# Windowed attention and two MLPs: in the last Winograd sweep ScalarE copies both accumulator banks, an adding DMA joins them in DRAM, and the plan gets new lengths and a new order

## The chip, the cores and the metric

The kernel runs on one core of a Trainium2 chip. The metric is the device time of one execution in microseconds. Before the change it was 630.57 us (median of three runs, 630.27 to 630.82).

## What is computed

Three stages follow each other over 2304 tokens (4 sequences of 576) of 512 features, in float32:

```python
scores = scale * q @ k.T                       # 4 x 8 heads, 576 x 576, 64 per head
attn   = softmax(where(0 <= i - j < 64, scores, -1e9)) @ v
x      = attn as (2304, 512)
h      = maximum(x @ w_in, 0);  x = (h * h) @ w_out          # FFN1, 512 -> 2048 -> 512
h      = x @ w2_in                                           # FFN2, 512 -> 1024
solu   = h * softmax(h)
ln     = (solu - mean) / sqrt(var + 1e-6) * g_ln
out    = ln @ w2_out                                         # 1024 -> 512
```

## The kernel before

Every float32 product is made as three products of a high and a low part, so one block product is some multiple of three matmuls. FFN1 runs in passes over the tokens. The first pass multiplies plainly. The second and the last use Strassen-Winograd: seven half-size products in place of eight, with sums and differences of the operands made by VectorE (DVE).

**The last pass.** For each j of eight, the products of the first layer are followed by the parts of the second layer whose operands are at hand: P1, P2 and P4. The operands of the other four products are stored in DRAM. When the first layer is done, `swept()` runs the sweep: P5 (8 steps), P6 (8), P3 (8) and P7 (8). A step is six matmuls of 128x512. Its operand is read back from DRAM (line 1199 is the load), copied by ScalarE (ACT) as the high part (line 1091), subtracted by DVE for the low part (line 1094) and multiplied at line 1070. P1, P6 and P7 accumulate in one pair of PSUM banks ("b"), P5 and P3 in another ("a"), P4 in a third ("t"), P2 in a fourth.

**What leaves the sweep.** The four quarters of the result are sums of banks: c11 is P1 + P2, c12 is the P5/P3 bank plus a saved copy U2 of the P1/P6 bank, c21 is the P1/P6/P7 bank plus P4, and c22 is that bank plus a saved copy of P5. `out()` does it: ACT copies one bank to SBUF (line 1152, or `copied` at line 1174 for the saved ones), DVE adds the other bank to that copy (line 1157, eight adds in all), and SyncE (SP) stores the sum (line 1160). P6 continues in the banks of P1, so its first matmul waits until c11 has been added. The t banks of P4 are given back when c21 has been added, which is after P7.

**FFN2.** `pair2(n)` does nine pairs of token tiles, again by Winograd: seven products of six matmuls (line 1546), whose banks ACT copies (u2 at 1556, u4 at 1560, u5 at 1564; `xx` at 1521 are high parts of the operands), then softmax, LayerNorm and transposes through DRAM (`lnT`, lines 1696 and 1700), then 48 matmuls at line 1707. Pair 0 takes the a banks, pair 1 the t banks, pair 2 the b banks. The variance's root is taken by GpSimd (POOL, lines 1652 and 1653).

**What sets the order.** Nothing is left to a scheduler of the compiler. Each task is put into a `Plan` with an engine, a planned length, a rank, the buffers that it takes and gives, and a lateness (`late`: the time from the end of a DMA's issue to its planned landing). The plan lists the tasks by earliest start, then by rank; `SHIFT` corrects ranks by task number, and each engine gets its instructions in the order so found. 51 dummy matmuls ("warm", line 1782) of rank 900 fill what the plan sees as gaps of TensorE (PE).

Of the kernel before, what the change touches and what calls it, by code (L numbers as in the profile page):

```python
# [26 lines left out]
class Plan:  # L27
# [10 lines left out]
    SHIFT = {0: 13.59, 3: 4.48, 4: -11.32, 22: -7.17, 37: 14.79, 71: -15.08, 162: -5.57, 188: 6.06, 192: -3.28, 195: 10.82, 198: 10.82, 202: -1.28,  # L38
# [69 lines left out]
def kernel(  # L108
# [96 lines left out]
    with ExitStack() as c1:  # L205
# [20 lines left out]
        tops, turns = [], [0]  # L226

        def assembled(kind, i, rank, after=()):
# [22 lines left out]
            def top():  # L251
                if ringed:
# [593 lines left out]
        def w_operands(t, j, rank, after):  # L846
# [59 lines left out]
            kept_wo[j] = [add("SP", 1.6, rank + WOS, lambda o=o, k=k: kept(o, k), [x], late=2.5) for k, (o, x) in enumerate(((V_, v), (Y, y)))]  # L906
# [929 lines left out]
```

## Time and profile before

| | |
|---|---|
| median of three runs | 630.57 us |
| the profiled execution | 631.49 us |
| its span | 629.7 us |
| PE busy | 621.6 us |
| DVE busy | 484.6 us |
| ACT busy | 434.8 us |
| POOL busy | 45.3 us |

The profiled execution is 0.92 us above the median; its span leaves 1.8 us outside. In the rows further down, times are microseconds from the start of the span. A row of a timeline begins with the start and the duration of a run of like instructions, then engine, line, operation, tiles and count; a bracket at the end is the idle time ahead of it and what ended that. Consecutive matmuls overlap, so the pace of PE is read from start to start. L1070 is line 1070 of the code above.

### The profile page before, as it was taken

To read this page: it belongs to the slowest core of one execution; us is meant where nothing else is said; L and a number is where in the kernel's file an instruction comes from. 1 tells how busy PE (TensorE), PEld (TensorE's weight loads), DVE (VectorE), ACT (ScalarE), POOL (GpSimd) and SP (SyncE) were. 2 spreads that over 40 slices of the span, in tenths; PEclk is the share of its full clock that TensorE was granted. 3 is DMA by queue.
4 is the path that set the end of the run, shared out by engine and by line. 5 is a ranking of instruction groups with operands and counts; after the bars stand their busy time and mean duration, and the time that the engine had idled before them with its cause. 6 is when DMAs were issued, how large, how long until landed. Compare 5 with 4: busy or idle time off the path is not lost.

```text
span 629.7 us, 11572 instructions
## 1 busy us (share of the span) xinstructions
PE 621.6 (99%) x4009; PEld 523.7 (83%) x4009; DVE 484.6 (77%) x1129; ACT 434.8 (69%) x985; POOL 45.3 (7%) x80
## 2 busy tenths in 40 slices
PE   8999999999999999999999999999999999999998
PEld 4798878889999999998888887778778788888886
DVE  5999897497967652587899998998688976686440
ACT  5879785677877674638677767774688875776451
POOL 1000000001221110000000000000001010110010
DMA  8888979447899998946767557964166565532351
GB/s 274 287 305 278 310 252 326 128 173 264 247 351 312 336 304 271 337 155 230 236 251 263 203 195 235 328 208 138 68 184 206 181 199 167 197 137 86 116 184 50
DMA packets 85451, 141.27 MB, mean 224 GB/s; under 512 B 7824, under 2 KB 49552, under 8 KB 85392
## 3 DMA queue, kind: packets, MB, share of 16 engines
q1 hardware_dynamic: 84704, 140.14, 66.3%
q8 instruction: 31, 0.51, 0.3%
q10 hardware_dynamic: 688, 0.39, 0.2%
q14 instruction: 28, 0.23, 0.1%
HBM read 90.69 MB, written 49.81 MB: 223 GB/s over the span
## 4 chain that ended last, share of the span: by engine, by line
PE 86%; DVE 5%; DMA 4%; ACT 3%; issue 1%; SPq 1%; POOL 0%; ACTq 0%; DVEq 0%; POOLq 0%
PE ps_h L936 22%; PE ps_o L1707 14%; PE ps_y L1070 10%; PE ps_h L1546 10%; PE ps_y L1256 10%; PE ps_y L707 7%; PE ps_h L691 6%; PE ps_s L436 3%; PE ps_v L519 2%; PE ps_warm L1782 1%; DMA l<-t_dram 1%; DMA kt<-in_k 1%; DMA r_dram<-u 1%; DMA t_dram<-h 1%; PE ps_v L522 1%
## 5 line engine op out<-in xcount | busy, mean ns | idle before, releaser
L1707 PE MATMUL ps_o<-w2o,lnT 128*128 128x512 f32 x432 | 99.1, 389 | 0.0
L1707 PEld LDWEIGHTS ps_o<-w2o,lnT 128*128 128x128 f32 x432 | 81.1, 188 | 16.9
L1256 PE MATMUL ps_y<-g,wb 128*128 128x384 f32 x384 | 71.3, 336 | 0.4 <-ACT y L655 0.4
L1256 PEld LDWEIGHTS ps_y<-g,wb 128*128 128x128 f32 x384 | 66.6, 188 | 1.4 <-ACT y L655 0.7
L1546 PE MATMUL ps_h<-w2i,xx 128*128 128x512 f32 x243 | 62.8, 391 | 0.0
L1070 PE MATMUL ps_y<-g,wb 128*128 128x512 f32 x234 | 58.3, 391 | 1.1 <-DVE y L1157 1.0
L1546 PEld LDWEIGHTS ps_h<-w2i,xx 128*128 128x128 f32 x243 | 45.6, 188 | 9.6
L1070 PEld LDWEIGHTS ps_y<-g,wb 128*128 128x128 f32 x234 | 43.7, 188 | 11.4 <-DVE y L1157 1.4
L936 PE MATMUL ps_h<-xa,wo 128*128 128x512 f32 (+1 forms) x192 | 52.7, 369 | 0.0
L936 PE MATMUL ps_h<-xb,wo 128*128 128x384 f32 (+1 forms) x192 | 51.3, 358 | 0.0
L707 PE MATMUL ps_y<-g,wb 128*128 128x512 f32 (+1 forms) x240 | 48.2, 352 | 0.1
L691 PE MATMUL ps_h<-x,wa 128*128 128x512 f32 (+1 forms) x240 | 47.3, 351 | 0.0
L936 PE MATMUL ps_h<-xo,wo 128*128 128x512 f32 (+1 forms) x128 | 47.3, 369 | 0.0
L451 ACT ACTIVATE e<-e,nmax 128x128 f32<-128x128 f32 x112 | 43.3, 390 | 2.2 <-DVE nmax L440 2.2
L707 PEld LDWEIGHTS ps_y<-g,wb 128*128 128x128 f32 x240 | 38.5, 189 | 6.6 <-issue 0.7
L691 PEld LDWEIGHTS ps_h<-x,wa 128*128 128x128 f32 x240 | 38.5, 189 | 6.0 <-ACT g L637 0.2
L936 PEld LDWEIGHTS ps_h<-xa,wo 128*128 128x128 f32 x192 | 35.3, 188 | 5.2 <-DVE u L622 0.4
L1696 ACT ACTIVATE lnT<-l 128x512 fp32r<-128x512 f32 x36 | 22.2, 627 | 23.0 <-PE ps_o L1707 23.0
L1546 PE MATMUL ps_h<-w2x,xx 128*128 128x512 f32 x135 | 37.0, 393 | 0.9 <-ACT u L1560 0.7
L936 PEld LDWEIGHTS ps_h<-xb,wo 128*128 128x128 f32 x192 | 34.5, 188 | 3.9 <-issue 0.7
L640 DVE TENSOR_TENSOR g<-r,g 128x384 fp32r<-128x384 f32 (+2 forms) x36 | 20.4, 570 | 21.7 <-ACT g L637 21.7
L461 POOL TENSOR_TENSOR e<-e,sums 128x512 f32<-128x512 f32 x16 | 18.5, 1179 | 205.0 <-PE ps_h L936 141.9
(182 smaller groups left out, 1267.7 us busy)
## 6 DMA issues: line engine op xcount, KB each, us to landing
wraw<-in_w_in SPq DMA_DIRECT2D x24, 511.8 KB, 5.3
wraw<-in_w_out SPq DMA_DIRECT2D x24, 511.8 KB, 4.8
vt<-in_v SPq DMA_DIRECT2D x32, 256.0 KB, 4.3
wo_dram<-wo SPq DMA_DIRECT2D x16, 512.0 KB, 5.4
wo<-wo_dram SPq DMA_DIRECT2D x16, 512.0 KB, 4.9
t_dram<-h SPq DMA_DIRECT2D x16, 512.0 KB, 2.9
l<-t_dram SPq DMA_DIRECT2D x64, 128.0 KB, 2.9
kt<-in_k SPq DMA_DIRECT2D x16, 384.0 KB, 5.2
```

Source lines behind the costliest of these rows:

```text
L436: T.matmul(to, qt[rows, i, hp, :], kt[rows, keys, hp, :], start=not begins, stop=not begins or hp == hps[-1])
L451: S.activation(out=o["er"][:, a, w], in_=s, func=AF.Exp, scale=SCALE if begins else -1.0, bias=o["nmax"][:, a, w : w + 1], accum_out=o["su ...
L461: eng.tensor_tensor(out=o["er"][:, a], in0=o["er"][:, a], in1=o["sums"][:, a].unsqueeze(2).to_broadcast([P, HP, W]), op=ALU.mult)
L640: V.tensor_tensor(out=o["g"][:, 1, :N], in0=o["r"], in1=o["g"][:, 0, :N].bitcast(F32), op=ALU.subtract)
L691: T.matmul(ps[:, :N], wa[kk][:, wi, c * P : c * P + P], xs[t][:, xi, c, n0:n1], start=n == 0, stop=n == 3 * DC - 1)
L707: T.matmul(acc[t, 0][d][:, n0:n1], wb[kk][:, wi, d * P : d * P + P], o["g"][:, xi, :N], start=kk == 0 and n == 0 and n0 == 0, stop=last an ...
L936: T.matmul(to[:, :N], w["t"][:, wi, off + c * P : off + c * P + P], (lo if xi else hi)()[:, c], start=begins and m == 0, stop=m == 5, skip ...
L1070: T.matmul(acc[name][d][:, :N], wb[kk][:, wi, col + d * P : col + d * P + P], q["g"][:, xi, :N], start=j == 0 and n == 0 and name not in ( ...
L1256: T.matmul(acc[t, half][d][:, :N], wb[kk][:, wi, d * P : d * P + P], q["g"][:, xi, :N], start=pos == 0 and n == 0, stop=pos == KF - 1 and ...
L1546: T.matmul(o[bank], o["xx", k][:, xi, at : at + P], w2i[w, r][wi][0](), start=begins and m == 0, stop=m == 5, skip_group_check=True)
L1696: S.activation(out=parts2(o["l", hf][:, 0]), in_=turned2(hf), func=AF.Copy)
L1707: T.matmul(o["o"], o["l", hf][:, xi, kk % 4, :], w2o[kk][:, wi, :], start=kk == 0 and n == 0, stop=kk == KF2 - 1 and n == 2)
```

## The change

`out()` is replaced by three helpers. `taken()` lets ACT copy a bank to SBUF. `stored_as()` lets SP store such a copy plainly to its place in DRAM. `added_to()` lets POOL issue a DMA with `accum_op=ALU.add`, which adds the other copy to what lies there; it comes after the plain store has landed. All eight DVE adds vanish, ACT copies 14 banks where it copied 8, SP still issues eight stores, and POOL issues eight adding transfers of 128x512. The banks of P4 are given back as soon as ACT has copied them. Five planned latenesses grow, the two halves of a zeroed buffer (`top`) are handed out in the order in which they come free, and `SHIFT` is a new table, so that the plan comes out in another order nearly everywhere.

```diff
-    SHIFT = {0: 13.59, 3: 4.48, 4: -11.32, 22: -7.17, 37: 14.79, 71: -15.08, ...
+    SHIFT = {0: 13.59, 10: -12.41, 22: -7.17, 27: -14.74, 28: -9.14, ...
...
-        tops, turns = [], [0]
+        tops, turns = [], [0, 1]
...
-            kept_wo[j] = [add("SP", 1.6, rank + WOS, lambda o=o, k=k: kept(o, k), [x], late=2.5) ...
+            kept_wo[j] = [add("SP", 1.6, rank + WOS, lambda o=o, k=k: kept(o, k), [x], late=3.0) ...
...
-                r_ready[t, kk] = add("SP", 0.8, ..., late=LATE_R if t == 2 else 2.2, give=["wm"])
+                r_ready[t, kk] = add("SP", 0.8, ..., late=LATE_R + 0.45 if t == 2 else 2.2, give=["wm"])
...
-            kept_t[j, "T1"] = ... late=2.2 ...; kept_t[j, "B22"] = ... late=2.2 ...; kept_t[j, "T"] = ... late=2.5 ...
+            kept_t[j, "T1"] = ... late=2.65 ...; kept_t[j, "B22"] = ... late=2.65 ...; kept_t[j, "T"] = ... late=3.4 ...
...
-            def out(d, half, a, b, after, early=None, **kw):
+            def taken(bank, after, rank, **kw):
                 o = {}
                 def copy():
                     o["y"] = raw_p.tile([P, 512], F32, tag="wm", name="y", bufs=WMB)[:, :N]
-                    S.activation(out=o["y"], in_=b(), func=AF.Copy)
-                def evict():
...
-                    V.tensor_tensor(out=o["y"], in0=a(), in1=b() if early is None else o["y"], op=ALU.add)
-                def store():
-                    nc.sync.dma_start(out=x2_dram[t][:, d, half * N : half * N + N], in_=o["y"])
...
-                y = add("DVE", 0.68, r, evict, after, take=["wm"] * (early is None), **kw)
+                    S.activation(out=o["y"], in_=bank(), func=AF.Copy)
+                return o, add("ACT", 0.58, rank, copy, after, take=["wm"], **kw)
+            def stored_as(d, half, y, after, slot=("wm",)):
+                def store():
+                    nc.sync.dma_start(out=column(d, half), in_=y())
+                return add("SP", 0.8, begin + 50, store, after, late=2.2, give=list(slot))
+            def added_to(d, half, o, after, slot=("wm",)):
+                def grow():
+                    G.dma_start(out=column(d, half), in_=o["y"], accum_op=ALU.add)
+                stored.setdefault((t, half), []).append(add("POOL", 1.1, begin, grow, after, late=5.5, give=list(slot)))
...
-            c11 = [out(d, 0, bank_of("P1", d), bank_of("P2", d), done, done[1:], rank=begin - 20, give=["b"] * d) for d in range(2)]
+            for d in range(2):
+                o, e = taken(bank_of("P2", d), done[1:], begin - 20)
+                first.append(stored_as(d, 0, lambda o=o: o["y"], [e]))
+            for d in range(2):
+                o, e = taken(bank_of("P1", d), [*done, e], begin - 20, give=["b"] * d)
+                c11.append(e)
+                added_to(d, 0, o, [e, first[d]])
...
-            ys = [out(2 + d, 0, bank_of("P1", d), bank_of("P4", d), [p7], [p7, into["P4", last]], rank=begin, give=["t"]) for d in range(2)]
+                o, e = taken(bank_of("P4", d), [into["P4", last], e], begin, give=["t"])
+                y = stored_as(2 + d, 0, lambda o=o: o["y"], [e])
+                o, u = taken(bank_of("P1", d), [p7], begin, give=["b"] * d)
+                y = added_to(2 + d, 0, o, [u, y], ())
+                added_to(2 + d, 1, o, [u, s5[d], y])
```

Lines 1070, 1546 and 1782 of before are lines 1069, 1566 and 1802 now.

**Place 1: PE where the sweep begins.** `ps_y_3863` (now `ps_y_3857`) is the bank pair of P1, `ps_y_4806` and `ps_y_4807` (now `4837` and `4838`) are the banks of P5, `ps_y_3973` (now `3974`) is that of P2. Before:

```order
L1070 MATMUL ps_y_3863<-g_4708,wb_1747 128x512 x6
L1782 LDWEIGHTS ones_97
L1782 MATMUL ps_warm_4795<-ones_97 128x512
...
L1782 MATMUL ps_warm_4802<-ones_97 128x512
L1070 MATMUL ps_y_4806<-g_4779,wb_566 128x512 x3
L1070 MATMUL ps_y_4807<-g_4779,wb_566 128x512 x3
L1070 MATMUL ps_y_4806<-g_4772,wb_768 128x512 x3
L1070 MATMUL ps_y_4807<-g_4772,wb_768 128x512 x3
L1070 MATMUL ps_y_3973<-g_4799,wb_1778 128x512 x6
```

Three warm matmuls stand between the last step of P1 and the first of P5. Now:

```order
L935 MATMUL ps_h1_3754<-xb_3625,wz_4565 128x512 x6
L1069 MATMUL ps_y_3857<-g_4712,wb_1730 128x512 x6
L1802 LDWEIGHTS ones_97
L1802 MATMUL ps_warm_4793<-ones_97 128x512
...
L1802 MATMUL ps_warm_4834<-ones_97 128x512
L1069 MATMUL ps_y_4837<-g_4812,wb_568 128x512 x3
L1069 MATMUL ps_y_4838<-g_4812,wb_568 128x512 x3
L1069 MATMUL ps_y_3974<-g_4818,wb_1763 128x512 x6
L1069 MATMUL ps_y_4837<-g_4785,wb_731 128x512 x3
L1069 MATMUL ps_y_4838<-g_4785,wb_731 128x512 x3
```

There are 13 warm matmuls there now, and the eight steps of P5 stand ahead of the first step of P6; before, the first step of P6 stood behind the sixth of P5.

**Place 2: DVE at the same place,** from the operands of the first P5 steps to those behind the cuts of the last weight (`wf`, four instructions of 128x256). Before:

```order
L1094 TENSOR_TENSOR gx_4814<-r_4804,gx_4814 128x512
L1157 TENSOR_TENSOR y_4870<-ps_y_3863,y_4870 128x512
L1035 TENSOR_TENSOR wf_4847<-wf_4847 128x256
L1036 TENSOR_TENSOR wf_4847<-wf_4847 128x256
L1037 TENSOR_TENSOR wf_4847<-wf_4847 128x256
L1038 TENSOR_TENSOR wf_4847<-wf_4847 128x256
L1094 TENSOR_TENSOR gx_4814<-r_4817,gx_4814 128x512
L1094 TENSOR_TENSOR g_4887<-r_4842,g_4887 128x512
L1044 TENSOR_TENSOR wb_1747<-wf_4847,wb_1747 128x512
L1044 TENSOR_TENSOR wb_1778<-wf_4847,wb_1778 128x512
L1157 TENSOR_TENSOR y_4916<-ps_y_3863,y_4916 128x512
```

The two adds of c11 stand among the operands of the sweep. Now:

```order
L1093 TENSOR_TENSOR g_4860<-u1_4710,g_4860 128x512
L1034 TENSOR_TENSOR wf_4847<-wf_4847 128x256
L1035 TENSOR_TENSOR wf_4847<-wf_4847 128x256
L1036 TENSOR_TENSOR wf_4847<-wf_4847 128x256
L1037 TENSOR_TENSOR wf_4847<-wf_4847 128x256
L1093 TENSOR_TENSOR g_4883<-r_4832,g_4883 128x512
L1093 TENSOR_TENSOR g_4875<-r_4823,g_4875 128x512
L1093 TENSOR_TENSOR gx_4790<-r_4845,gx_4790 128x512
L1043 TENSOR_TENSOR wb_1730<-wf_4847,wb_1730 128x512
L1043 TENSOR_TENSOR wb_1763<-wf_4847,wb_1763 128x512
L335 TENSOR_TENSOR ws2_4923<-w2i_4798,ws2_4773 128x512
```

No add of banks is left, the cuts stand ahead of the operand of P5's third step (`g_4883`), and the weights of FFN2 (line 335) begin earlier. From the instruction that makes the last result of the first layer to the low part of P6's seventh operand (`g_5061`) there are 43 DVE instructions, four of them these cuts.

**Place 3: PE from the sweep to FFN2.** `ps_h2` are banks of FFN2: `ps_h2_5363` (now `5272`) is pair 1's in the t banks, `ps_h2_5260` and `5249` (now `5297` and `5286`) are pair 0's. Before:

```order
L1546 MATMUL ps_h2_5249<-w2i_5120,xx_5235 128x512 x3
L1070 MATMUL ps_y_3863<-g_5213,wb_1613 128x512 x6
L1070 MATMUL ps_y_3863<-gx_4814,wb_1747 128x512 x6
L1782 LDWEIGHTS ones_97
L1782 MATMUL ps_warm_5339<-ones_97 128x512
...
L1782 MATMUL ps_warm_5360<-ones_97 128x512
L1546 MATMUL ps_h2_5363<-w2i_4829,xx_5164 128x512 x3
L1546 MATMUL ps_h2_5363<-w2x_4901,xx_5164 128x512 x3
L1546 MATMUL ps_h2_5260<-w2i_4787,xx_5164 128x512 x3
```

Pair 0 stands between the sixth and the seventh step of P7, and seven warm matmuls stand between P7's last step and pair 1. Now:

```order
L1069 MATMUL ps_y_4838<-gx_4790,wb_1763 128x512 x3
L1566 MATMUL ps_h2_5272<-w2i_4921,xx_5186 128x512 x3
L1566 MATMUL ps_h2_5272<-w2x_4936,xx_5186 128x512 x3
L1566 MATMUL ps_h2_5286<-w2i_4921,xx_5214 128x512 x3
...
L1566 MATMUL ps_h2_5286<-w2i_5045,xx_5267 128x512 x3
L1069 MATMUL ps_y_3857<-g_5270,wb_1227 128x512 x6
L1069 MATMUL ps_y_3857<-g_5228,wb_1400 128x512 x6
L1069 MATMUL ps_y_3857<-g_5283,wb_1561 128x512 x6
L1069 MATMUL ps_y_3857<-gx_4790,wb_1730 128x512 x6
L1566 MATMUL ps_h2_5297<-w2i_4904,xx_5186 128x512 x3
```

The first product of pair 1 now stands ahead of pair 0, right behind the last step of P3; four steps of P7 follow pair 0, and the other six products of pair 1 follow them without a warm matmul. Of the 51 warm matmuls 38 now stand early, around the first attention units, 13 at the start of the sweep and none behind it; before it was 36, 3, and 12 behind it (7 here, 1 between pairs 1 and 2, 4 at the end of the kernel).

Two more moves have no rows here. Ahead of the last products of pair 2, ACT's order is now the copy u2, one `lnT`, the copy u4, where it was u2, two `xx`, u4. At the start of the kernel SP issues the first weight load (512 KB) as its second DMA, ahead of the second half of q and of the `qk` loads of the second attention unit, where it came after them.

## Rows read from the trace of the kernel before

**Rows 1.** The page, busy time, share of the span and instructions of each engine:

```profile
PE 621.6 (99%) x4009; PEld 523.7 (83%) x4009; DVE 484.6 (77%) x1129; ACT 434.8 (69%) x985; POOL 45.3 (7%) x80
```

**Rows 2.** Windows: length, busy PE, PEld, DVE, ACT, POOL; granted clock; DMA share; GB/s:

```profile
396.00:416.00 20.00, 18.57 (x78) 13.84 (x76) 19.86 (x36) 14.58 (x27) 0.00 (x0) 1.00 0.88 297
...
447.50:470.00 22.50, 21.69 (x94) 16.67 (x94) 19.41 (x48) 17.06 (x29) 1.49 (x4) 1.00 0.47 153
```

**Rows 3.** Timeline of PE in the sweep:

```profile
388.06 0.82 PE L1782 MATMUL ps_warm<-ones 128*128 128x512 bf16 x3
...
397.10 1.75 PE L1070 MATMUL ps_y<-gx,wb 128*128 128x512 f32 x7
399.02 1.42 PE L1070 MATMUL ps_y<-gx,wb 128*128 128x512 f32 x5 [0.17 <-DVE gx L1094]
401.42 1.66 PE L1070 MATMUL ps_y<-g,wb 128*128 128x512 f32 x6 [0.98 <-DVE y L1157]
...
414.84 0.40 PE L1070 MATMUL ps_y<-gx,wb 128*128 128x512 f32 x1
```

**Rows 4.** Timeline of PE from the last step of P7 to the fourth pair:

```profile
447.52 2.12 PE L1782 MATMUL ps_warm<-ones 128*128 128x512 bf16 x7
449.29 1.04 PE L1546 MATMUL ps_h<-w2i,xx 128*128 128x512 f32 x3
...
465.43 2.20 PE L1546 MATMUL ps_h<-w2i,xx 128*128 128x512 f32 x9
468.33 0.96 PE L1546 MATMUL ps_h<-w2x,xx 128*128 128x512 f32 x3 [0.70 <-ACT u L1560]
...
469.82 11.04 PE L1707 MATMUL ps_o<-w2o,lnT 128*128 128x512 f32 x48
480.70 0.84 PE L1546 MATMUL ps_h<-w2i,xx 128*128 128x512 f32 x3
...
490.73 1.55 PE L1707 MATMUL ps_o<-w2o,lnT 128*128 128x512 f32 x6
```

**Rows 5.** Timeline of DVE in the sweep and behind it:

```profile
385.99 0.68 DVE L622 CUSTOM_DVE_ANT_0 u<-ps_h,u 128x512 f32<-128x512 f32 x1
...
396.56 0.42 DVE L1035 TENSOR_TENSOR wf<-wf 128x256 f32<-128x256 f32 x1
...
398.28 0.69 DVE L1094 TENSOR_TENSOR gx<-r,gx 128x512 fp32r<-128x512 f32 x1
...
448.25 1.28 DVE L1157 TENSOR_TENSOR y<-ps_y,y 128x512 f32<-128x512 f32 x2
```

**Rows 6.** Timeline of ACT ahead of the last products of FFN2's pair 2:

```profile
466.86 0.93 ACT L1521 ACTIVATE xx<-xr 128x512 fp32r<-128x512 f32 x2
467.69 0.59 ACT L1560 ACTIVATE u<-ps_h 128x512 f32<-128x512 f32 x1
468.17 1.15 ACT L1696 ACTIVATE lnT<-l 128x512 fp32r<-128x512 f32 x2
```

**Rows 7.** ACT's groups by line: count, busy, mean ns of one, idle before:

```profile
L1152 ACT ACTIVATE y<-ps_y 128x512 f32<-128x512 f32 x4 | 2.2, 586 | 0.5 <-DVE g L1094 0.5
```

**Rows 8.** Timeline of DVE beside POOL's work:

```profile
163.73 0.37 DVE L878 TENSOR_TENSOR ws<-w,ws 128x256 f32<-128x256 f32 x1
...
165.50 1.26 DVE L881 TENSOR_TENSOR ws<-w,ws 128x256 f32<-128x256 f32 x1
```

**Rows 9.** Timeline of POOL at the same time:

```profile
163.99 2.49 POOL L461 TENSOR_TENSOR e<-e,sums 128x512 f32<-128x512 f32 x2 [3.62 <-DVE sums L457]
```

**Rows 10.** DMA issues from 385 to 452 us: count, KB, median us to landing:

```profile
x_dram<-y SPq DMA_DIRECT2D x8, 256.0 KB, 3.8
xr<-x_dram SPq DMA_DIRECT2D x6, 256.0 KB, 3.6
```

**Rows 11.** DMA issues from 0 to 25 us, the same columns:

```profile
wraw<-in_w_in SPq DMA_DIRECT2D x4, 511.8 KB, 7.6
```

**Rows 12.** Timeline of PE at the start:

```profile
8.12 0.46 PE L436 MATMUL ps_s<-qk 64*64 64x64 f32 x16 [0.19 <-DMA qk<-in_k]
```

More of the change, by code (lines that the diff above doesn't have):

```diff
@@ L905, in w_operands @@
             z = cut(Z, lambda: units()[:, 3], 256, have)
-            kept_wo[j] = [add("SP", 1.6, rank + WOS, lambda o=o, k=k: kept(o, k), [x], late=2.5) for k, (o, x) in enumerate(((V_, v), (Y, y)))]
+            kept_wo[j] = [add("SP", 1.6, rank + WOS, lambda o=o, k=k: kept(o, k), [x], late=3.0) for k, (o, x) in enumerate(((V_, v), (Y, y)))]
             return named(u, v, y, z, [u, v2, v4, z])
@@ L1005, in pair1 @@
                 f = squared(Named({}, o, x), N, rank(k) + 14.3, [f], False, False)
-                r_ready[t, kk] = add("SP", 0.8, rank(k) + 3, lambda x=x, kk=kk: store(x, kk), [f], late=LATE_R if t == 2 else 2.2, give=["wm"])
+                r_ready[t, kk] = add("SP", 0.8, rank(k) + 3, lambda x=x, kk=kk: store(x, kk), [f], late=LATE_R + 0.45 if t == 2 else 2.2, give=["wm"])
             for x, kk, f, slot, k, seconds in (("c11", 2 * j, f11, "r", 1, (10, 11) if lastj else (10, 13)), ("c12", 2 * j + 1, f12, "wm", 9, (12, 13) if lastj else (16, 19))):
@@ L1145, in swept, with column @@
             outs = {}
-            def out(d, half, a, b, after, early=None, **kw):
+            def column(d, half):
+                return x2_dram[t][:, d, half * N : half * N + N]
+            def taken(bank, after, rank, **kw):
                 o = {}
@@ L1151, in copy @@
                     o["y"] = raw_p.tile([P, 512], F32, tag="wm", name="y", bufs=WMB)[:, :N]
-                    S.activation(out=o["y"], in_=b(), func=AF.Copy)
-                def evict():
-                    if early is None:
-                        o["y"] = raw_p.tile([P, 512], F32, tag="wm", name="y", bufs=WMB)[:, :N]
-                    V.tensor_tensor(out=o["y"], in0=a(), in1=b() if early is None else o["y"], op=ALU.add)
-                def store():
-                    nc.sync.dma_start(out=x2_dram[t][:, d, half * N : half * N + N], in_=o["y"])
-                r = kw.pop("rank")
-                if early:
-                    after = [*after, add("ACT", 0.58, r, copy, early, take=["wm"])]
-                y = add("DVE", 0.68, r, evict, after, take=["wm"] * (early is None), **kw)
-                stored.setdefault((t, half), []).append(add("SP", 0.8, begin + 50, store, [y], late=2.2, give=["wm"]))
-                return y
+                    S.activation(out=o["y"], in_=bank(), func=AF.Copy)
+                return o, add("ACT", 0.58, rank, copy, after, take=["wm"], **kw)
+            def stored_as(d, half, y, after, slot=("wm",)):
+                def store():
+                    nc.sync.dma_start(out=column(d, half), in_=y())
[4 more added lines that the diff above has]
+                stored.setdefault((t, half), []).append(add("POOL", 1.1, begin, grow, after, late=5.5, give=list(slot)))
+                return stored[t, half][-1]
             def copied(name, key, rank, after):
@@ L1212, in swept @@
             k5 = copied("P5", "P5", begin, [p5])
+            s5 = [stored_as(2 + d, 1, lambda d=d: saved("P5", d)(), [k5], ["raw"] * d) for d in range(2)]
             for i in range(last + 1):
@@ L1215, in swept @@
             k2 = past["U2"] = copied("P1", "U2", begin, [p6])
+            s2 = [stored_as(d, 1, lambda d=d: saved("U2", d)(), [k2], ["raw"] * d) for d in range(2)]
             for i in range(last + 1 + LEAD2):
```

22 lines of the change are left out of this document (14 added, 8 removed), and 13 rows, old and new, of the table SHIFT.

## The prediction

> **What bounds the kernel now.** I read the page first, then the windows by stage, then PE's timeline from the sweep to FFN2, and for each gap the timeline of the engine that ended it. PE is busy for 621.6 of 629.7 us [rows 1], and no stage shows it idle for long, so the kernel is PE's work plus small losses. A loss is seen only from start to start. 48 matmuls of 128x512 run from 469.82 to 480.70, which is 0.2267 us for one [rows 4], 1.36 us for a step of six. By that pace I count what PE loses where the change works.
>
> In the sweep, from 388.06 to 414.84 [rows 3], PE runs 102 such matmuls, 23.1 of 26.8 us. **3.7 us are lost**: three warm matmuls (0.76), the start of P6 (1.60: seven plus five matmuls take from 397.10 to 401.42; the bracket names DVE's add at line 1157 for 0.98), and small waits. In that stretch DVE is busy for 19.86 of 20 us, ACT for 14.58 [rows 2]: DVE sets the pace of the operands, and each DVE instruction taken from there is worth something.
>
> In the transition, from 447.52 to 490.73 [rows 4], PE runs 174 matmuls, 39.4 of 43.2 us. **3.8 us are lost**: seven warm matmuls, 1.77 us by the next start, while pair 1 waits for the t banks that DVE's adds give back (they run from 448.25, [rows 5]); then 0.86 where pair 2 waits for ACT's copy u4 (nine matmuls from 465.43 should have ended 2.04 us later, the next begins at 468.33); the rest in pieces of 0.1 to 0.4, among them one warm matmul.
>
> **The change part by part.**
>
> The eight DVE adds go. Each takes 0.60 us from start to start (two in 1.28 with their overlap, [rows 5]). The six copies more on ACT cost 0.59 each [rows 7], 3.5 us of ACT in a stretch where it was busy for 73% [rows 2]. That hides them as long as ACT's order doesn't put one ahead of an operand that PE is short of; each such place costs up to 0.6.
>
> *Sweep.* The 13 warm matmuls are a fixed price now: 13 x 0.2267 = 2.95 us, where before three cost 0.76. What they cover is DVE's chain. Call T the end of the first layer's last product. Before, T was 385.34, two steps of 1.36 ahead of the warm matmuls at 388.06 [rows 3], and DVE's last result of that layer began 0.65 behind it, at 385.99, and took 0.60 [rows 5]. Its end, T + 1.25, is the anchor. The first operand of P5 is the fifth DVE instruction behind it: T + 4.3. PE reaches P5 at 1.36 (the last step of P1) + 2.95, T + 4.3. They meet. Up to P6's seventh operand there are 43 DVE instructions: 39 of 0.60 and four cuts that take 1.72 together (396.56 to 398.28, [rows 5]), 25.1 us, so it is ready at T + 26.4 if DVE never waits. PE gets there 16 steps after P5's start, at T + 26.1. So PE still waits there for 0.3 to 0.5 us, and for as much more as DVE waits itself. Before, DVE waited for 0.14 in 20 us. Now ACT has more to do and the FFN2 weights, whose loads DVE needs, are mixed in earlier, so I allow DVE 0 to 1.5 us. Loss in the sweep: 2.95 + 0.5 to 2.95 + 2.0, taken at 4.0 since DVE has had almost no wait there. Against 3.7 before, **+0.3 (−0.2 to +1.3)**. The wait of P6 for c11 is gone, but it has been paid in advance by the warm matmuls.
>
> *Transition.* The t banks are free once ACT has copied P4, which is done long before P3 ends, so pair 1's first product starts ahead of pair 0 and the 1.77 go to zero. The other copies that pair 0 needs (the a banks behind P3) are covered by that product, 1.36 us against two copies of 0.59. The copy u4 stands behind one `lnT` (0.52) and no longer behind two `xx` (0.83, [rows 6]): 0.86 becomes 0.55. The single warm matmul goes. New is that pair 2's operands are made by DVE between pair 1's evictions and softmax, in a stretch where DVE is busy for 19.41 of 22.5 us [rows 2]; pair 2 starts some two steps sooner after them, and I allow 0 to 0.7. Loss afterwards 0.7 to 2.1, taken at 1.4. Against 3.8: **−2.4 (−3.1 to −1.7)**.
>
> *Start and end.* The 512 KB weight load goes ahead of the second half of q and of the second unit's `qk`. Those 512 KB take 7.6 us to land beside the rest [rows 11], and PE already waits for `qk` at 8.12, though for 0.19 only [rows 12]. If the small loads land later by the time of 512 KB at the 297 GB/s that the DMAs move elsewhere [rows 2], that is 1.7 us at most; the weight itself comes sooner, which can give a little back. Warm matmuls stand in the same stretch and swallow a shift. I take **+0.2 (−0.5 to +1.0)**. The four warm matmuls of the end go; they filled a wait for other engines, so nothing is won. What the new order does elsewhere I take at nothing.
>
> *Adding transfers.* POOL has nothing to do there, so issuing is free. The landing isn't: an adding transfer holds its `wm` buffer, and behind the first two an SP load for P3 waits for that buffer, with the rest of SP's queue. No row shows such a transfer. A plain store lands after 3.8, a store and a read together take 7.4 [rows 10]. The code plans 1.1 for the issue and 5.5 for the landing, and SP's order follows that. At 7.4 in place of 6.6 the third step of P3 would be late by up to 0.8, at 3.8 by nothing; I take nothing, as in the landing nearest to it, and keep 0.8 for the range.
>
> The Trainium skill ("DMA: Bandwidth & Descriptors", section "Anatomy of one DMA — SWDGE (gpsimd) path") gives such a transfer about 2.0 us and its bytes at 436 GB/s. By that page my estimate for 256 KB is 2.6 us, below both rows, and the sum would stay as it is. No run so far shows it.
>
> Sum: +0.3 − 2.4 + 0.2 = **−1.9 us**. On the profiled execution, 631.49, that is 629.6; the median of the runs lies 0.92 lower, so **628.7**.
>
> **The rivals.**
>
> *A, taken back.* DVE's chain waits for ACT and for loads after all (sweep +1.3), pair 2 waits for its operands (transition −1.7), the start takes 0.2: −0.2 us, 630.4, no change. For it: the margin between PE and DVE in the sweep is 0.3 us wide, and where PE is pulled forward by two steps in the transition, DVE and ACT are busy for 86% and 76%. Against it: eight DVE instructions less.
>
> *B, slower: the adding transfers disturb DVE.* Their issue is POOL's work, and POOL and DVE can hold each other up: a DVE instruction of 128x256 took 0.37 alone and 1.26 while POOL multiplied two SBUF tiles [rows 8, 9]. If each of the eight issues cost DVE such a hold of 0.6 to 1.0 us on the path, 4.8 to 8.0 us would come on top of −1.9: 633.5 to 636.7. If only the two in DVE's full stretch and one in the transition count, 1.8 to 3.0: 630.5 to 631.7. It decides against the change from 0.4 us for each of the eight. Against it: in those rows POOL reads SBUF operands itself, and here it only issues.
>
> The Trainium skill ("SBUF — State Buffer", section "Who interferes with whom") says that a DVE instruction with two SBUF inputs is held up by a POOL instruction that reads SBUF, not by one that only writes, and that DVE's two-port modes can starve POOL's descriptor making. The rows agree with its first half; by the second half the price would fall on the transfers' landing, not on DVE. That lowers B's chance here, not to zero.
>
> *C, all of it.* DVE never waits, the start gains, pair 2's operands are in time: −0.2 − 3.1 − 0.5 = −3.8, 626.8.
>
> That the change does less than it says (the t banks still held, or P6 still late) would show as 1.8 or 1.0 us kept; the order rules the first out, and with the second alone the time is 629.7, between the forecast and A.
>
> **How the numbers follow.** A measurement of this kernel can tell some 0.2%, 1.26 us, from no change: faster is below 629.3, slower above 631.8. Forecast (628.7) 0.46, C (626.8) 0.11, A (630.4) 0.27, B and a late landing (above 631.8) 0.16. So faster 0.57, same 0.27, slower 0.16. The range leaves out half of C's tail and most of B: 626.6 to 631.8.
>
> **What would show it.** Right: no bracket with a DVE add in PE's rows; 13 warm matmuls, then P5 with waits of 0.3 us or less; P6's steps at 1.36 but for one wait of about 0.5 near the seventh; P7's last four steps, six products of pair 1 and pair 2 without a gap above 0.6; DVE as before in its instructions' lengths while POOL issues. Wrong: DVE instructions of 1 us and more beside POOL's issues (B); an SP load that sits behind an adding transfer, and P3 waiting for its operand; waits of P5 and P6 that add up to over 2 us (A); or a first product of FFN1 that comes a microsecond later than before.

## The result and the profile after

The changed kernel takes **635.14 us** (633.25 to 636.89, six runs), the kernel before 630.89 beside it (six runs): a ratio of 1.0068, 95% interval 1.0050 to 1.0087. It is slower by 4.25 us, where 1.9 less were forecast, and it lies outside the range.

The profiled execution took 636.00 us (span 634.2), that of before 631.49. Counted as in the prediction, start to start against 0.2267 us for a matmul, the 4.5 us between them lie here (the end of P7 is the border of sweep and transition, the second group of `mm_o` at 494.80, before 490.73 [rows 4], that of the transition):

| part | before | after | difference | forecast |
|---|---|---|---|---|
| up to the warm matmuls of the sweep, at equal work (387.22, before 388.06 [rows 3]) | | | −0.84 | +0.2 |
| lost in the sweep, P5 to P7 | 3.66 | 8.35 | +4.69 | +0.3 |
| lost in the transition | 3.77 | 3.99 | +0.22 | −2.4 |
| behind the second `mm_o` | | | +0.43 | 0 |

PE's timeline of the changed kernel in the sweep (start, busy us, line, tiles, count, idle before and what ended it), to be held against [rows 3]:

```profile
387.22 3.20 PE L1802 MATMUL ps_warm<-ones 128*128 128x512 bf16 x13
390.36 7.25 PE L1069 MATMUL ps_y<-g,wb 128*128 128x512 f32 x30
...
403.33 1.55 PE L1069 MATMUL ps_y<-g,wb 128*128 128x512 f32 x6
405.57 3.01 PE L1069 MATMUL ps_y<-g,wb 128*128 128x512 f32 x12 [0.70 <-ACT y L1154]
...
413.87 0.39 PE L1069 MATMUL ps_y<-g,wb 128*128 128x512 f32 x1
415.25 2.06 PE L1069 MATMUL ps_y<-g,wb 128*128 128x512 f32 x6 [0.99 <-DVE g L1093]
417.53 2.79 PE L1069 MATMUL ps_y<-g,wb 128*128 128x512 f32 x11 [0.22 <-DVE g L1093]
...
422.86 4.15 PE L1069 MATMUL ps_y<-gx,wb 128*128 128x512 f32 x17 [0.81 <-DVE gx L1093]
```

Read it by starts. The warm matmuls take 3.14. Then PE waits at P6's first step (six matmuls from 403.33 should end at 404.69, the next begins at 405.57; with the slower restart 0.97), at P6's seventh step (1.26), its eighth (0.90) and P3's third (1.19). P5's last step but one adds 0.42, small pieces 0.47: 8.35. Who is late is seen one engine further back. ACT's timeline in the same stretch:

```profile
402.04 0.60 ACT L1154 ACTIVATE y<-ps_y 128x512 f32<-128x512 f32 x1 [2.40 <-DVE gx L1093]
...
404.93 0.59 ACT L1154 ACTIVATE y<-ps_y 128x512 f32<-128x512 f32 x1
...
416.12 0.63 ACT L1090 ACTIVATE g<-r 128x512 fp32r<-128x512 f32 x1 [1.44 <-DMA r<-tt_dram]
...
419.65 0.63 ACT L1090 ACTIVATE gx<-r 128x512 fp32r<-128x512 f32 x1 [1.93 <-DMA r<-r_dram]
```

P6's first step waits for a *copy* of c11 by ACT (line 1154) where it waited for a DVE add before [rows 3]. Behind the seventh step the late operands come from rounding (line 1090) whose read-back loads have not landed. DVE, beside POOL's issues and ahead of them:

```profile
400.11 0.69 DVE L335 TENSOR_TENSOR ws<-w2i,ws 128x512 f32<-128x512 f32 x1 [1.58 <-DMA tt_dram<-tt]
...
408.49 0.68 DVE L1093 TENSOR_TENSOR gx<-r,gx 128x512 fp32r<-128x512 f32 x1
409.09 0.68 DVE L345 TENSOR_TENSOR w2x<-ws,w2x 128x512 fp32r<-128x512 f32 x1
409.69 0.68 DVE L335 TENSOR_TENSOR ws<-w2i,ws 128x512 f32<-128x512 f32 x1
```

POOL's timeline at that time:

```profile
408.64 1.98 POOL L1168 DMA_DIRECT2D x_dram<-y  x2 [54.03 <-ACT w2x L342]
```

POOL issues two adding transfers from 408.64 to 410.62, and DVE's instructions keep their 0.68 beside them. But DVE stood still for 1.58 up to 400.11, waiting for the store of `tt`; from 396 to 416 it is busy for 17.34 of 20 us, where it was 19.86 before [rows 2]. SP's queue, its timeline and its waits from 385 to 475 us (waited for: us in total, times, longest):

```profile
402.76 0.96 SPq L1161 DMA_DIRECT2D x_dram<-y  x2
408.11 0.32 SPq L1203 DMA_DIRECT2D r<-tt_dram  x1
...
412.54 4.10 SPq L1203 DMA_DIRECT2D r<-r_dram  x3
```

```profile
SPq L1203 <- DMA x_dram<-y: 10.5, 5, 4.3
```

The same view of before:

```profile
SPq L1199 <- DMA x_dram<-y: 3.0, 2, 2.1
```

The kernel has four `wm` buffers. ACT's copies, the read-back loads of the odd operands and other steps take turns in them, and a copy holds its buffer until its transfer has landed. SP therefore stands for 10.5 us on loads whose buffer a copy still holds, and everything behind them stands too: nothing is issued from 403.7 to 408.1. That longest wait, 4.3, is for a plain store: SP issued it at 402.76, and it landed at 408.04, before POOL's first adding transfer was issued. How long the transfers take (DMA issues from 385 to 440 us: count, KB, median us to landing), after:

```profile
r<-tt_dram SPq DMA_DIRECT2D x16, 256.0 KB, 4.6
r<-r_dram SPq DMA_DIRECT2D x12, 256.0 KB, 4.7
...
x_dram<-y SPq DMA_DIRECT2D x4, 256.0 KB, 5.4
x_dram<-y POOLq DMA_DIRECT2D x4, 256.0 KB, 6.3
```

and before:

```profile
r<-tt_dram SPq DMA_DIRECT2D x16, 256.0 KB, 3.7
r<-r_dram SPq DMA_DIRECT2D x12, 256.0 KB, 3.7
```

Over this stretch adding transfers land after 6.3 us, and the read-back loads after 4.6 and 4.7 where it was 3.7. The median of 6.3 hides two pairs: the two adding transfers in the sweep, which hold `wm` buffers while P3 needs loads, take 7.66 and 8.00, the two behind P3 4.20 and 4.89. The issues from 400 to 425 us alone:

```profile
x_dram<-y POOLq DMA_DIRECT2D x2, 256.0 KB, 7.8
```

The two `xr` loads that SP issues right behind them, at 411.00 and 411.63, land after 7.14 and 7.27.

Last the transition, PE's timeline (to [rows 4]) and ACT's:

```profile
451.33 1.52 PE L1069 MATMUL ps_y<-gx,wb 128*128 128x512 f32 x6
452.69 2.20 PE L1566 MATMUL ps_h<-w2i,xx 128*128 128x512 f32 x9
...
465.38 0.98 PE L1566 MATMUL ps_h<-w2x,xx 128*128 128x512 f32 x3 [0.29 <-ACT p L1572]
...
470.89 0.97 PE L1566 MATMUL ps_h<-w2x,xx 128*128 128x512 f32 x3 [1.10 <-ACT u L1580]
...
491.93 1.65 PE L1566 MATMUL ps_h<-w2i,xx 128*128 128x512 f32 x6 [1.40 <-DVE nmax L1595]
```

```profile
469.72 0.63 ACT L1716 ACTIVATE lnT<-l 128x512 fp32r<-128x512 f32 x1 [0.59 <-DMA l<-t_dram]
470.26 0.58 ACT L1580 ACTIVATE u<-ps_h 128x512 f32<-128x512 f32 x1
...
489.31 1.15 ACT L1716 ACTIVATE lnT<-l 128x512 fp32r<-128x512 f32 x2 [1.33 <-DMA l<-t_dram]
```

The seven warm matmuls are gone and pair 1 follows P7 without a gap. But `lnT` waits for its load, and the copy u4 (line 1580) stands behind it: 1.37 lost with the restart, where before it was 0.97. ACT's `p` costs another 0.56 at 465.38. The same happens at 489.31, and through DVE's own `lnT` add behind that, `nmax` of pair 3 is late and 1.67 are lost at 491.93.

### The profile page after: what moved, and what is told of

It is laid out like the page before. It is cut to its first block, busy times and chain, and to the rows that moved or that the text cites. A ratio compares the mean times of both kernels' runs of the same rounds, so it can differ in the third digit from the quotient of the medians.

```text
span 634.2 us, 11609 instructions
## 1 busy us (share of the span) xinstructions
PE 621.1 (98%) x4009; PEld 523.4 (83%) x4009; DVE 479.2 (76%) x1121; ACT 439.6 (69%) x991; POOL 53.7 (8%) x88
## 4 chain that ended last, share of the span: by engine, by line
PE 85%; DMA 7%; DVE 4%; ACT 1%; issue 1%; SPq 1%; POOL 0%; ACTq 0%; POOLq 0%; DVEq 0%
PE ps_h L935 22%; PE ps_o L1727 14%; PE ps_y L1276 11%; PE ps_h L1566 10%; PE ps_y L1069 9%; PE ps_h L690 6%; PE ps_y L706 5%; PE ps_s L435 3%; PE ps_v L518 2%; DMA l<-t_dram 1%; PE ps_warm L1802 1%; DMA t_dram<-h 1%; DMA wraw<-in_w_out 1%; DMA r<-r_dram 1%; PE ps_v L521 1%
```

## The experiments

My theory after this reading: the loss is waits, made by buffers that are held until a transfer lands and by an order in which instructions that wait for a transfer stand ahead of those that PE needs. Rivals: (i) POOL's transfers disturb DVE; (ii) the new order alone is bad, or the new way alone; (iii) the adding itself, with its long landing, is the price whatever the buffers. "Lost" is always PE's loss from the first layer's last product to the second `mm_o` in the profiled execution (before 7.45, after 12.37). Times are medians, and ratios go against runs of the kernel before on the same chip; "lost" is of one execution each. In the edits, `ahead(n, m)` puts task n right ahead of task m in the finished list of the plan.

| kernel | us | ratio to before, 95% | lost |
|---|---|---|---|
| new_way_old_order | 643.61 | 1.0204 (1.0189 to 1.0219) | 20.97 |
| old_way_new_order | 639.81 | 1.0146 (1.0129 to 1.0163) | |
| own_p1_p4 | 634.83 | 1.0082 (1.0052 to 1.0111) | 11.23 |
| no_add | 633.35 | 1.0040 (1.0026 to 1.0054) | 9.84 |
| tt_early | 636.14 | 1.0087 (1.0058 to 1.0115) | 11.93 |
| ffn2_swaps | 635.66 | 1.0072 (1.0051 to 1.0094) | 12.23 |
| three_warm | 634.05 | 1.0050 (1.0033 to 1.0066) | 10.56 |
| own_tt | 634.08 | 1.0046 (1.0032 to 1.0060) | 10.01 |
| own_tt_xr | 633.61 | 1.0048 (1.0031 to 1.0064) | 9.39 |
| after_all | 633.90 | 1.0053 (1.0038 to 1.0069) | 8.82 |
| full_add | 633.69 | 1.0045 (1.0029 to 1.0060) | 9.03 |
| full_plain | 631.33 | 1.0010 (0.9998 to 1.0021) | 7.53 |
| before_8_less | 629.04 | 0.9974 (0.9965 to 0.9983) | 5.61 |
| before_three | 628.56 | 0.9964 (0.9952 to 0.9977) | 5.26 |

**new_way_old_order**: the changed kernel with the table, latenesses and turns of before.

```diff
-    SHIFT = {0: 13.59, 10: -12.41, 22: -7.17, 27: -14.74, ...
+    SHIFT = {0: 13.59, 3: 4.48, 4: -11.32, 22: -7.17, ...
...
```

> The copies and adding transfers of the changed kernel, with the rank corrections, planned latenesses and buffer turns of the kernel before. Theory 1 (the four wm buffers, held by the copies until stores and adding transfers have landed, keep SP's read-back loads waiting): slower than before by 2 to 5 us, 633 to 636, with PE waiting in the sweep for operands whose loads come late. Theory 2 (the new order alone costs it): no slower than before, 629 to 631.5.

Measured 643.61. PE's timeline at P6's first step:

```profile
403.18 1.43 PE L1062 MATMUL ps_y<-g,wb 128*128 128x512 f32 x5 [0.74 <-DVE g L1086]
410.88 1.65 PE L1062 MATMUL ps_y<-g,wb 128*128 128x512 f32 x3 [6.27 <-ACT y L1147]
```

PE waits for 6.27 us for a copy of c11: in the old order it comes far too late. The time is above what either theory expected.

**old_way_new_order**: the kernel before with the new table, latenesses and turns.

```diff
-    SHIFT = {0: 13.59, 3: 4.48, 4: -11.32, 22: -7.17, ...
+    SHIFT = {0: 13.59, 10: -12.41, 22: -7.17, 27: -14.74, ...
...
```

> The kernel before with its eight DVE adds, but with the rank corrections, planned latenesses and buffer turns of the changed kernel. Theory 1 (wm buffers): within 1.5 us of before, 629 to 632. Theory 2 (the order): slower by 3 us or more, 634 to 637.

Measured 639.81, with a wait of 4.73 us for `lnT` at 465.54 and one of 2.8 for a DVE operand that ends at 411.65. About 3 us of the loss is the clock: behind each of these two waits some 3.4 us stand at a granted clock of 0.5, and about seven matmuls take 0.2 longer each; new_way_old_order has two such stretches too, 6.8 us from 406.9 and 3.4 from 427.4. Each half alone is slower than both together, so the crossing can't divide the loss between order and way. Rival (ii) is not settled by it, and the other runs edit the kernels in small pieces.

**own_p1_p4**: the copies of P1 (c11) and P4 go to the buffers of q and k, which are idle then, not to `wm`.

```diff
-                    o["y"] = raw_p.tile([P, 512], F32, tag="wm", name="y", bufs=WMB)[:, :N]
+                    if own:
+                        o["y"] = at_p.tile([P, 512], F32, tag=own, name="y", bufs=1)[:, :N]
+                    else:
+                        o["y"] = raw_p.tile([P, 512], F32, tag="wm", name="y", bufs=WMB)[:, :N]
...
-                o, e = taken(bank_of("P1", d), [*done, e], begin - 20, give=["b"] * d)
+                o, e = taken(bank_of("P1", d), [*done, e], begin - 20, own="qk"[d], give=["b"] * d)
...
-                o, e = taken(bank_of("P4", d), [into["P4", last], e], begin, give=["t"])
+                o, e = taken(bank_of("P4", d), [into["P4", last], e], begin, own="qk"[d], give=["t"])
```

> The changed kernel in its own order, but ACT's copies of P1 (for c11) and of P4 go to two buffers that lie idle in the sweep (those of q and k), so that four of the ten copies no longer hold a wm buffer. Theory 1: SP's wait for wm buffers falls from 10.5 us to under half, the sweep gets back 2 to 4 of its 4.7 us, 631 to 633.5. Theory 2: within 1 us of the changed kernel, 634 to 636.

Measured 634.83. SP's wait for `x_dram<-y`, 10.5 before the edit, is gone from its list, and with it P6's eighth step (0.90) and P3's third (1.19). This shows that the held buffers made these two. But DVE now waited for 2.83 for the store of `tt`, and P5's last step but one lost 1.65: of 2.1 removed, 1.1 is left as a gain in the profile, and the median hardly moves, where 631 to 633.5 were expected of the buffers.

**no_add**: plain stores in place of the adding transfers, which leaves the sums of the two banks out.

```diff
-    G.dma_start(out=column(d, half), in_=o["y"], accum_op=ALU.add)
+    G.dma_start(out=column(d, half), in_=o["y"])
```

> The changed kernel with POOL's eight transfers as plain stores in place of adding ones, so the four quarters of the last pass come out as one bank each and not as sums. If adding itself is slow (theory 3: the transfer reads the place before it writes), the landing falls from 5.2 us to about 4 and the time by 1 us or more, 634 or less. If not, landing and time stay within 0.5 us, 634.5 to 636.

Measured 633.35. DMA issues from 385 to 440 us, and those from 400 to 425 alone:

```profile
r<-tt_dram SPq DMA_DIRECT2D x16, 256.0 KB, 4.8
r<-r_dram SPq DMA_DIRECT2D x12, 256.0 KB, 4.6
...
x_dram<-y POOLq DMA_DIRECT2D x4, 256.0 KB, 3.6
```

```profile
x_dram<-y POOLq DMA_DIRECT2D x2, 256.0 KB, 4.6
```

The same bytes land after 3.6 us as against 6.3, and the ratio falls from 1.0068 to 1.0040: 1.8 us, and the intervals still overlap by a little. Over the whole stretch the read-back loads land as late as with adding transfers (4.8 and 4.6 as against 4.6 and 4.7), so it isn't the adding that takes them there from 3.7. What the adding delays is what is issued right behind it: the two `xr` loads there take 3.90 and 4.99 here, 7.14 and 7.27 in the changed kernel. SP's wait for held buffers falls from 10.5 only to 7.8, and its longest part, 4.3 for the plain store, stays.

**tt_early**: SP's store of `tt` six of its instructions earlier.

```diff
+    order.remove(at_[1503])
+    order.insert(order.index(at_[1497]) + 1, at_[1503])
```

> The changed kernel with one transfer moved in SP's order: the last store of operands that the sweep reads back (tt, 512 KB) is issued six SP instructions earlier, as soon as it is written. In the changed kernel DVE's first sum of FFN2 weights (line 335) stands in DVE's queue and waited 1.58 us until that store had landed, because it takes over its buffer. Theory 2a (this one wait in DVE's queue makes P6's first and seventh step late): the wait goes, PE's waits at P6's first step (0.86) and seventh (1.15) shrink to under 0.5 together, 1.3 to 2 us off, 633 to 634. Theory 1 (wm buffers alone): DVE's wait goes, PE's waits stay, within 0.6 us of the changed kernel, 634.5 to 636.

Measured 636.14, no gain. DVE's 1.58 and P6's first wait are gone, as they should; P6's seventh step, which was to shrink with them, still loses 1.08 of its 1.26. P3's third step then waits for 2.22 in two pieces, and SP for 12.0 on the held buffers.

**ffn2_swaps**: ACT's u4 ahead of one `lnT`, DVE's first eviction of pair 3 ahead of two `lnT` adds.

```diff
+    ahead(1904, 1816)
+    ahead(1958, 1877)
```

> The changed kernel with two neighbours swapped in FFN2: ACT copies u4 of pair 2 ahead of the lnT part that waits for its transfer, and DVE evicts c11 of pair 3 ahead of the two lnT parts that wait for ACT. Theory 2b (the new order puts instructions that wait for a transfer ahead of those that PE needs): PE's waits there (1.26 and 1.56) fall under 0.6 each, 1.5 to 2.2 us off, 633 to 634. If instead what PE waits for is late by itself: the waits move by no more than 0.5 each, within 0.8 us of the changed kernel.

Measured 635.66, no change. The 1.37 for u4 are gone, but 1.29 for ACT's p (line 1572) come at 489.10, and of the 1.67 for `nmax` 1.28 stay.

**three_warm**: ten of the 13 warm matmuls left out.

```diff
+    spare_ = [t for t in order if t["rank"] == 900.0 and 300 < t["start"] < 400][3:]
+    plan.order = [t for t in order if t not in spare_]
```

> The changed kernel without ten of the thirteen warm matmuls at the start of the sweep, all else in its order. If they only cover a wait for DVE's operands of P5 (as the prediction has it): PE waits there instead, and the time stays within 0.5 us of the changed kernel. If they delay PE by themselves: up to 2.3 us off, 633 or less.

Measured 634.05. PE's timeline, and windows (length, busy PE, PEld, DVE, ACT, POOL; granted clock; DMA share; GB/s):

```profile
388.34 0.50 PE L1069 MATMUL ps_y<-g,wb 128*128 128x512 f32 x1 [0.68 <-ACT g L1090]
389.65 6.68 PE L1069 MATMUL ps_y<-g,wb 128*128 128x512 f32 x21 [0.80 <-DVE g L1093]
```

```profile
390.50:394.00 3.50, 3.50 (x10) 2.76 (x9) 3.47 (x7) 1.15 (x2) 0.00 (x0) 0.52 0.86 238
```

The ten take 2.27 us. PE loses 1.04 between the three and P5's first matmul and 1.19 behind it, 2.23 together, of which 0.2 is a slow start that the 13 have as well: the 13 warm matmuls covered a real wait for operands. Then eight matmuls run at 0.43 us each, at a granted clock of 0.52 (the level of 1.2 GHz), which costs 1.6 more. The kernel is not slower all the same (1.0050 as against 1.0068, with intervals that overlap), and its profile loses 1.8 less. That comes from later: with operands that much further ahead of PE, P6's first step waits for 0.30 in place of 0.97, and P5's wait and that of P6's eighth step are gone.

**before_8_less**: the kernel before without the seven warm matmuls ahead of pair 1 and the one behind it.

```diff
+    spare_ = [t for t in order if t["rank"] == 900.0 and 430 < t["start"] < 460][0:]
+    plan.order = [t for t in order if t not in spare_]
```

> The kernel before without its seven warm matmuls behind P7 and the one behind pair 1, all else in its order. The prediction said that they stand in for a wait until DVE's adds give back the t banks. If so, PE waits there instead and the time stays within 0.5 us of before, 630.3 to 631.3. If the banks are in truth free when ACT has copied P4 and the eight are only the plan's guess: up to 2.0 us off, 628.7 to 629.7.

Measured 629.04, faster than before by 1.6 us. Timelines of ACT, PE and DVE where pair 1 begins:

```profile
446.87 1.06 ACT L1152 ACTIVATE y<-ps_y 128x512 f32<-128x512 f32 x2
```

```profile
447.36 1.52 PE L1070 MATMUL ps_y<-gx,wb 128*128 128x512 f32 x6
448.72 0.84 PE L1546 MATMUL ps_h<-w2i,xx 128*128 128x512 f32 x3
```

```profile
449.45 1.28 DVE L1157 TENSOR_TENSOR y<-ps_y,y 128x512 f32<-128x512 f32 x2
```

Pair 1 begins in the t banks at 448.72 without a wait, before DVE's adds begin. The banks were free as soon as ACT had copied P4. The seven warm matmuls were only filler that the plan had put there.

**own_tt**, **own_tt_xr**, **after_all**: sets. The first is own_p1_p4 with tt_early; the second adds this, SP's two `xr` loads behind six read-back loads of P3 and P7:

```diff
+    ahead(1824, 1604)
```

the third is own_tt with 8 warm matmuls and five swaps in FFN2:

```diff
+    ahead(1904, 1816)
+    ahead(1958, 1877)
+    ahead(1960, 1876)
+    ahead(1956, 1932)
+    ahead(1896, 1795)
+    spare_ = [t for t in order if t["rank"] == 900.0 and 300 < t["start"] < 400][8:]
```

> The changed kernel with two edits together that won nothing alone: ACT's copies of P1 and P4 in the idle buffers of q and k, and the tt store six SP instructions earlier. Theory 4 (the sweep has two chains of nearly equal length, DVE behind the tt store and SP behind the wm buffers, so that removing one shows the other): together 2 to 3.5 us off the changed kernel, 631.5 to 633. Theory 5 (its losses have yet another cause): within 1 us of it, 634.2 to 636.

> own_tt with one more move in SP's order: the two loads of FFN2's operands (xr), which stand ahead of seven read-back loads of the sweep, behind them. In own_tt those two waited in SP's queue for a buffer and the loads behind them landed after 5.9 us in place of 3.7 before; PE then lost 1.03 us at P3's third step. Theory 6 (the last chain of the sweep is SP's order and the pile of transfers behind it): that wait falls under 0.4, landing under 5 us, 0.6 to 1.2 us off own_tt, 632.9 to 633.5. If the pile itself is the cause: the wait stays above 0.7 and the time within 0.5 us of own_tt, 633.6 to 634.6.

> own_tt, with five warm matmuls fewer at the start of the sweep (8 of 13 left) and five neighbours swapped in FFN2 (ACT's u4 of pair 2 and u5 of pair 3 ahead of lnT parts that wait for a transfer, its copy p of pairs 2 and 3 ahead of LayerNorm's squares, DVE's c11 of pair 3 ahead of lnT). If the order's waits are each local: the sweep and the transition lose 6 to 8 us in place of 12.4, 629.5 to 631.5, no slower than before. If FFN2 is late by its transfers all the same: 632 to 634.

Measured 634.08, 633.61 and 633.90. Edits that gave nothing one by one gain 0.9 to 1.4 us by the ratios together, with intervals that still overlap with the changed kernel's. The profiles say the same: own_p1_p4 loses 1.14 less than the changed kernel and tt_early 0.44 less, own_tt 2.36 less, so these two waits had covered each other in part. In own_tt_xr P3's third step lost its wait, as expected (0.13 where own_tt has 1.02), but the time did not follow: beyond own_tt nothing more comes out in the medians, though the profiles lose less (10.01, 9.39, 8.82).

**full_add** and **full_plain**: all of these edits at once, with adding transfers and with plain stores.

> The changed kernel with every edit of the runs so far that took a wait away: the copies of P1 and P4 in the buffers of q and k, the store of tt six SP instructions earlier, the loads of xr behind the read-backs of P3's operands, 8 warm matmuls ahead of P5 in place of 13, and the five swaps in FFN2. If the time is made of the waits named so far, about 8.2 us stay lost between the first layer's last product and the second group of mm_o (8 warm matmuls with P5's first wait 2.6, P6's seventh step 0.7, small waits of the sweep 1.2, FFN2 about 2.1, restarts of 0.11 for the rest) and the time is 631.4 to 632.5. If the landing times themselves (adding transfers in the same queue pair as the loads) set what DVE gets, new waits of a microsecond appear elsewhere in P6 and P3 and it is 633.5 to 634.5, as after each of the smaller sets of edits.

> The same, with the eight adding transfers of POOL as plain stores of the same bytes, which leaves the sums of the two banks out. If the adding itself still costs time once no copy holds a shared buffer, this run is faster than the one with adding transfers by 1 to 2 us (no_add was 1.8 below the changed kernel). If the buffers were the whole price of the adding, the two are within 0.5 us of each other. Below the kernel before (under 630) only if the other waits are short as well.

Measured 633.69 and 631.33: 2.36 us for the adding alone, with intervals that don't meet. PE's timeline of full_add, and then of full_plain, in P3 and P7, whose steps alternate there:

```profile
419.55 4.15 PE L1069 MATMUL ps_y<-gx,wb 128*128 128x512 f32 x17 [0.35 <-DVE gx L1093]
...
428.71 3.47 PE L1069 MATMUL ps_y<-gx,wb 128*128 128x512 f32 x14 [0.71 <-DVE gx L1093]
```

```profile
418.50 5.60 PE L1069 MATMUL ps_y<-gx,wb 128*128 128x512 f32 x24
...
428.60 3.71 PE L1069 MATMUL ps_y<-gx,wb 128*128 128x512 f32 x15 [0.20 <-DVE gx L1093]
```

DMA issues from 385 to 440 us, full_add and then full_plain:

```profile
r<-r_dram SPq DMA_DIRECT2D x12, 256.0 KB, 5.7
...
x_dram<-y POOLq DMA_DIRECT2D x4, 256.0 KB, 4.5
```

```profile
r<-r_dram SPq DMA_DIRECT2D x12, 256.0 KB, 4.5
...
x_dram<-y POOLq DMA_DIRECT2D x4, 256.0 KB, 2.4
```

The two adding transfers ahead of these waits read from the buffers of q and k, not from `wm`, so held buffers don't explain the difference: beside adding transfers the read-back loads from `r_dram` land later (5.7 as against 4.5; those from `tt_dram` take 5.3 in both), and PE waits for them. The three loads that SP issues next behind the two adding transfers take 5.8, 5.7 and 5.9 as against 2.6, 2.7 and 4.2. Theory and rival (iii) both hold a part. All edits together with plain stores take the loss away, clear of noise (1.0068 to 1.0010). How it divides is less sure: of the 4.25 us, the edits of order and buffers give back some 1.45 (ratio 1.0068 to 1.0045, intervals that overlap), the adding is 2.36 of what is then left, and 0.5, which can't be told from none, is the rest.

**before_three**: the kernel before, without the eight warm matmuls, with u4 ahead of the two `xx`, and c11's second copy and add earlier, its copy in q's buffer.

```diff
+            c11 = [out(d, 0, bank_of("P1", d), bank_of("P2", d), done, done[1:], own="q" * d, rank=begin - 20, give=["b"] * d) for d in range(2)]
...
+    ahead(1565, 1510)
+    ahead(1566, 1511)
+    ahead(1898, 1941)
+    spare_ = [t for t in order if t["rank"] == 900.0 and 430 < t["start"] < 460][0:]
+    plan.order = [t for t in order if t not in spare_]
```

> The kernel before with three local edits and no adding transfer: without the eight warm matmuls behind P7; ACT's u4 of pair 2 ahead of the two xx; and the second copy and add of c11 ahead of the last weight's parts, its copy in the idle buffer of q. If each wait is what it looks like in the trace: 1.8, 0.5 to 0.8 and 0.6 to 1.1 us off, 627 to 628.2. If the next wait takes them: 628.5 to 629.3, as without the eight warm matmuls alone.

Measured 628.56, below both kernels, 2.0 us under before. P6's first wait (1.25 with its restart) and u4's (0.97) are gone, most of that comes back in other places of 0.3 to 0.7 each, and the edits beyond before_8_less are worth 0.35 in the profile. With local edits on both sides, full_add (1.0045) stands further above before_three (0.9964) than the changed kernel above before: the edits narrow the loss only against the kernel before as it was.

## Why the prediction was wrong

**Sweep, forecast +0.3, came out +4.7.** The count of DVE's instructions was right, and it put a wait of 0.5 to 2.0 at P6's seventh step, where 1.26 came. That the size fits is in part luck: DVE waited for 2.4 us on the way (1.58 for the store of `tt`, 0.58 and 0.26 for ACT), more than the 1.5 allowed, and PE was late as well, at T + 28.0 in place of T + 26.1 (T is 385.86 here). The warm matmuls cost 3.14 as against 2.95, and three_warm shows that they cover a wait for DVE's chain, as the anchor T + 4.3 had it. The step that failed is "that hides them" for ACT's six copies more. I priced a copy by ACT's time alone, and of that there was enough (busy for 15.31 of 20 us from 396 to 416). What a copy also takes is a `wm` buffer until its transfer has landed, and own_p1_p4 shows two waits, 2.1 us, that go with it. The other half of the step's condition, "as long as ACT's order doesn't put one ahead of an operand", looked at the wrong side: the copy of c11 itself became the gate of P6's first step (0.97), since it stood behind instructions that waited for DVE, and DVE for the store of `tt`. tt_early shows that link.

**Adding transfers, forecast 0 (kept 0.8).** I took the landing nearest to a row of before, 3.8. For the two in the sweep it was 7.66 and 8.00, above the 7.4 of both rows of [rows 10] together, for which I had foreseen a delay of 0.8 at one step of P3. The mistake was to count one transfer and one step: loads issued behind the adding transfers land later too. By no_add and the full pair the adding costs 1.8 to 2.4 us. Apart from that, eleven transfers of 256 KB more are issued from 385 to 440 us (four adding ones, four stores and three weight loads that now come sooner), and the read-back loads land 0.9 to 1.0 later, with plain stores as well; that the number of transfers does this is likely, but no run varied it alone.

The Trainium skill ("DMA: Bandwidth & Descriptors", section "Anatomy of one DMA — SWDGE (gpsimd) path") led to an estimate of 2.6. A plain store by POOL took 2.4 in full_plain and 3.6 in no_add, near it; an adding one took 4.5 to 6.3, which that figure doesn't cover (medians from 385 to 440 us).

**Transition, forecast −2.4, came out +0.2.** The 2.0 us for warm matmuls did go. Two things were wrong behind that. The premise that pair 1 waits for DVE's adds is refuted by before_8_less: the same gain is to be had in the kernel before, so it is no gain of the change's way. And u4 was priced by one `lnT` of 0.52 in place of two `xx`; I did not ask whether that `lnT` waits for its load. It did (0.59 at 469.72, 1.33 at 489.31), and where I allowed 0 to 0.7 for pair 2's operands, pair 2 lost 0.56 at ACT's `p` and pair 3, for which I had allowed nothing, 1.67 at `nmax`. ffn2_swaps shows that taking one of these away lets the next wait decide.

**Start and end, +0.2.** The first product of FFN1's first stage begins at 21.77 where it was 21.38, 0.4 later and inside the bounds. At the sweep the kernel is 0.84 ahead all the same, but among the kernels with the new order the end of the first layer's last product lies anywhere from 385.0 to 387.3 in their profiles, and with the old order from 384.6 to 386.5, so this gain is no property that I can show. The 0.43 at the end were put at nothing with the four warm matmuls; no run took them apart.

**Rivals.** B's range held the time and its mechanism is false: DVE's instructions keep 0.68 beside POOL's issues. The Trainium skill ("SBUF — State Buffer", section "Who interferes with whom") said that a DVE instruction with two SBUF inputs is held up by POOL's reading of SBUF; issuing alone does not do that here, and the rows agree. The landing, which I had added to B's 0.16 with no price but the 0.8, was the real cost of the adding, 1.8 to 2.4. A named the places (DVE waiting for loads, pair 2 for its operands) and was too small by the number of them.

What stays open: why beyond own_tt the medians no longer follow the profiles, and why several kernels of the new way scatter by 3 to 4.4 us from run to run where before scatters by less than 2. Many waits of nearly equal length that hang on landings would do both, but no run shows it.

## What to carry to other kernels

An instruction taken from a busy engine is not free on an idle one: ask which buffer its result takes, until which transfer lands, and who is next for that buffer and queued behind it. Before an instruction is called cover, look whether it waits for a transfer itself. And try the gain alone before it is credited to the change: eight filler matmuls, taken out of the kernel before, were worth more than the whole rebuild.

## What the chip showed that I had not expected

An adding DMA lands much later than a plain one of the same bytes in the same place: 6.3 as against 3.6 us, and 4.5 as against 2.4 in the full pair. POOL needs about 1 us to issue one (1.98 for two; the plain ones of no_add took 0.54 to 0.75 each). The loads that SP issues right behind one are delayed with it (`xr` 7.14 and 7.27 as against 3.90 and 4.99).

Two waits of 0.68 and 0.80 us on PE, 1.3 us apart, were followed by 3.5 us at a granted clock of 0.52, with a matmul at 0.43 us in place of 0.2267 (three_warm). Longer single waits (1.10 and 1.40 us in the changed kernel) were not followed by such a stretch; still longer ones of 2.79 and 4.73 in old_way_new_order were (3.4 us at 0.50 from 411.4, 3.5 us at 0.51 from 466.0). Filler that covers a wait can so be worth more than the wait: in that profile 1.6 us of slower matmuls came on top of the 2.23 of waiting, though the kernel as a whole was no slower without it.
